# Aligned load targets, one output store, and half of a weight piece loaded by 8 DMA engines, in a one-core decode layer

## The chip, the core and the metric

The kernel runs on one NeuronCore of one Trainium2 chip. The metric is the device time of one execution, in microseconds (us). The kernel before takes 216.2 us (median of 4 runs, 216.03 to 216.39). SP, ACT, PE, DVE and POOL are the core's sync, scalar, tensor, vector and GpSimd engines; SP and ACT issue the loads and stores here. Where the text says 8 or 16 engines, or the late ones, it means the 16 DMA engines over which the profile gives its DMA share. A landing is one of the semaphore records with which a load or store reports its data as done: 16 for a load of a whole K, V, wo or w4 piece, fewer for some others (one more record that those have, at most 1.1 us after the start of the issue, is not counted). I read one landing as one engine's share; the end of the kernel before, below, fits that, but no record names an engine. The eviction is the copy of the result from PSUM to SBUF.

## The reference, cut to what matters

```python
def reference(A_x, A_k_cache, A_v_cache, A_wq, A_wo, B_x, B_w1, B_w2, B_w3, B_w4):
    # attention of 4 decode tokens, 32 query heads over 16 KV heads, last 2048 positions of the cache
    # q = (x @ wq); p = softmax(q k^T / sqrt(128)); o = p v; return o @ wo      wo: [4096, 576]
    # MLP: x + gelu(layernorm(x1) @ w3) @ w4        w3: [576, 4608], w4: [4608, 576]
    x = A_x
    xn = _layernorm(x, axis=-1)
    return x + _A_ref(xn, A_k_cache, A_v_cache, A_wq, A_wo) + _B_ref(xn, B_w1, B_w2, B_w3, B_w4)
```

With one position per token, the shifted-window part of the MLP adds nothing, so w1 and w2 are not read. All inputs are bf16. There are 16 K tiles and 16 V tiles of 2 MB each (one per KV head, for all four tokens), 4.7 MB each of wq and wo, and 5.3 MB each of w3 and w4.

## The kernel before

Loads go out on one queue, issued by SP, in a fixed order: x, wq, K0 to K2, then wo pieces, V and K tiles in turn, w3 after V2, and w4 last. A KV tile has 128 partitions of 16 KB; seven such buffers let SP issue far ahead of need (a K load lands a median of 29.3 us after its issue).

```python
    x_bf = const.tile([B, D], BF16)
    nc.sync.dma_start(out=x_bf[:], in_=x2)
    for j in range(KJ):                                  # wq: 4 pieces of 8192 B per partition
        nc.sync.dma_start(out=wq_sb[:, j * NQ:(j + 1) * NQ], in_=wq_main[:, j, :])
    ...
    wo_src = A_wo.rearrange("(s p i) n -> s p (i n)", p=P, i=WOR)     # WOR = WOH = 8

    def load_kv(kind, h):                                # source dimensions 32 x 4 x 8192
        t = kvp.tile([P, NC, Dh], BF16, tag="kv", name=f"{kind.lower()}n")
        nc.sync.dma_start(out=t[:].rearrange("p c d -> p (c d)"),
                          in_=win[:, h].rearrange("b (p c) d -> p b (c d)", c=NC))

    def load_wo(p):                                      # 128 partitions of 9216 B
        t = wop.tile([P, WOR, D], BF16, tag="wo", name="wo_sb")
        nc.sync.dma_start(out=t[:].rearrange("p i n -> p (i n)"), in_=wo_src[p])

    W4_PIECES = [0, NFH // 2, NFH, NFH + 9, NFH + 14, NF]             # rows of 1152 B; NFH = 18
```

In a wo piece, the 1024 rows belong to 8 heads of 128 channels. Partition p holds 8 consecutive rows, so the attention output has to be spread over the partitions in the same order. Eight matmuls with selection matrices do that (`o_spread`), and a mask keeps each partition's own head (`o_pick`). Whoever changes where the rows of a piece land must change both. The result is accumulated in four blocks of PSUM partitions and stored by four DMAs, two issued by SP and two by ACT:

```python
    fin = const.tile([P, CW], out.dtype)
    nc.vector.tensor_copy(out=fin[:], in_=acc[:])
    for i in range(NQD):
        eng = nc.sync if i % 2 == 0 else nc.scalar
        eng.dma_start(out=o2[:, i * CW:(i + 1) * CW], in_=fin[i * QD:i * QD + B, :])
```

Of the kernel before, what the change touches and what calls it, by code (L numbers as in the profile page):

```python
# [9 lines left out]
ALU = mybir.AluOpType  # L10
AX = mybir.AxisListType
BF16 = mybir.dt.bfloat16
F32 = mybir.dt.float32
I32 = mybir.dt.int32
PSUM = bass.MemoryType.PSUM

NKV = 7
BIG = 1.0e30


@with_exitstack
def kernel(
# [14 lines left out]
    nc = tc.nc  # L37
    P = 128
    B, Sq, D = A_x.shape
    _, Hkv, Sk, Dh = A_k_cache.shape  # L40
    Hq = A_wq.shape[1] // Dh
# [4 lines left out]
    KJ = 4  # L46
    NQ = Hq * Dh
    NF = F // P
    NFH = NF // 2
# [3 lines left out]
    QD = 32  # L53
    NQD = P // QD
    CG = NC // NQD
    NSL = 4
    SC = NC // NSL
    CW = D // NQD
# [7 lines left out]
    x2 = A_x.flatten_outer_dims()  # L66
    o2 = out.flatten_outer_dims()
# [2 lines left out]

    ctx.enter_context(tc.manual_schedule())

    const = ctx.enter_context(tc.tile_pool(name="const", bufs=1))
    small = ctx.enter_context(tc.tile_pool(name="small", bufs=2))
    kvp = ctx.enter_context(tc.tile_pool(name="kv", bufs=NKV))
    ktp = ctx.enter_context(tc.tile_pool(name="kt", bufs=3))
    ptp = ctx.enter_context(tc.tile_pool(name="pt", bufs=3))
    wp = ctx.enter_context(tc.tile_pool(name="w", bufs=1))
    wop = ctx.enter_context(tc.tile_pool(name="wo", bufs=2))
    ps_s = ctx.enter_context(tc.tile_pool(name="ps_s", bufs=3, space=PSUM))  # L80
    ps_o = ctx.enter_context(tc.tile_pool(name="ps_o", bufs=2, space=PSUM))
    ps_m = ctx.enter_context(tc.tile_pool(name="ps_m", bufs=1, space=PSUM))
    ps_acc = ctx.enter_context(tc.tile_pool(name="ps_acc", bufs=1, space=PSUM))


    x_bf = const.tile([B, D], BF16)
    nc.sync.dma_start(out=x_bf[:], in_=x2)

    wq_main = A_wq[0:KJ * P, :].rearrange("(p j) n -> p j n", j=KJ)
    wq_sb = wp.tile([P, KJ * NQ + NQ // 2], BF16, tag="w", name="wq_sb")  # L90
    for j in range(KJ):
        nc.sync.dma_start(out=wq_sb[:, j * NQ:(j + 1) * NQ], in_=wq_main[:, j, :])
    nc.sync.dma_start(out=wq_sb[:, KJ * NQ:], in_=A_wq[KJ * P:D, :].rearrange("r (e f) -> (r e) f", e=2))

    w_tiles = {}
    wo_tiles = {}
    kv_tiles = {}
    WOH = 8
    WOR = WOH
    WOD = P // WOH  # L100
    WOQ = WOH // rep
    wo_src = A_wo.rearrange("(s p i) n -> s p (i n)", p=P, i=WOR)

    def load_kv(kind, h):
# [3 lines left out]
                          in_=win[:, h].rearrange("b (p c) d -> p b (c d)", c=NC))  # L108
        kv_tiles[kind, h] = t

    def load_wo(p):
        t = wop.tile([P, WOR, D], BF16, tag="wo", name="wo_sb")
        nc.sync.dma_start(out=t[:].rearrange("p i n -> p (i n)"), in_=wo_src[p])
        wo_tiles[p] = t

    def load_w3():
# [4 lines left out]
        nc.sync.dma_start(out=t[:, KJ * F:], in_=B_w3[KJ * P:D, :].rearrange("r (e f) -> (r e) f", e=2))  # L121
        w_tiles["w3"] = t

    W4_PIECES = [0, NFH // 2, NFH, NFH + 9, NFH + 14, NF]

    def load_w4():
        t = wp.tile([P, NF, D], BF16, tag="w", name="w4_sb")
# [7 lines left out]
    ident_bf = const.tile([P, P], BF16)  # L135
    make_identity(nc, ident_bf[:])
    ident_f = const.tile([P, P], F32)
# [3 lines left out]
    neg_half = const.tile([B, 1], F32)  # L141
    nc.gpsimd.memset(neg_half[:], -0.5)

    AB = ps_acc.tile([P, 512], F32)
    nc.vector.memset(AB[:], 0.0)
    q_ps = AB[:, 0:Hq * B].rearrange("p (h b) -> p h b", b=B)
    g_ps = AB[:, Hq * B:Hq * B + NF * B].rearrange("p (f b) -> p f b", b=B)
    acc = ps_acc.tile([P, CW], F32)
# [18 lines left out]
    def transposed(src_bf, name):  # L167
        dup = small.tile([B, 2, P], BF16, tag="dup")
        nc.vector.memset(dup[:], 0.0)
        for e in range(2):  # L170
            nc.vector.tensor_copy(out=dup[:, e, e:P:2], in_=src_bf[:, KJ * P:D])
        T = const.tile([P, KJ + 2, B], BF16, name=name)
        tp = ps_m.tile([P, KJ + 2, B], BF16, tag="m")
        for j in range(KJ):
            nc.tensor.transpose(out=tp[:, j, :], in_=src_bf[:, j:KJ * P:KJ], identity=ident_bf[0:B, 0:B])
        for e in range(2):
            nc.tensor.transpose(out=tp[:, KJ + e, :], in_=dup[:, e, :], identity=ident_bf[0:B, 0:B])
        nc.vector.tensor_copy(out=T[:], in_=tp[:])
        return T

    xn_f = const.tile([B, D], F32)
    xn_bf = const.tile([B, D], BF16)
    layernorm(xn_f, xn_bf, x_bf)
    xnT = transposed(xn_bf, "xnT")


    for j in range(KJ):
        for h in range(Hq):
            nc.tensor.matmul(out=q_ps[:, h, :], lhsT=wq_sb[:, j * NQ + h * Dh:j * NQ + (h + 1) * Dh],
                             rhs=xnT[:, j, :], start=False, stop=False, skip_group_check=True)  # L190
    for h in range(Hq):
        e, f0 = divmod(h * Dh, NQ // 2)
        nc.tensor.matmul(out=q_ps[:, h, :], lhsT=wq_sb[:, KJ * NQ + f0:KJ * NQ + f0 + Dh],
                         rhs=xnT[:, KJ + e, :], start=False, stop=False, skip_group_check=True)
# [4 lines left out]
    for kb in range(NQD):  # L199
        nc.vector.tensor_copy(out=sel[:, :, :, kb, :],  # L200
                              in_=ident_bf[:].rearrange("p (ib i e) -> p ib e i", ib=2, e=2))
    qs_ps = ps_m.tile([P, 2, 2, Hkv, rep, B], F32, tag="m")
    for ib in range(2):
        for e in range(2):
            nc.tensor.matmul(out=qs_ps[:, ib, e].rearrange("p h r b -> p (h r b)"),
                             lhsT=sel[:, ib, e].rearrange("p k i -> p (k i)"), rhs=q_bf[:], start=True, stop=True)
    qz = const.tile([P, Hkv, 2, 2, NQD, B, rep], BF16)
    nc.gpsimd.memset(qz[:], 0.0)
    for kb in range(NQD):
        for ie in range(4):  # L210
            ib, e = divmod(ie, 2)
            nc.vector.tensor_copy(out=qz[kb * QD:(kb + 1) * QD, :, ib, e, kb, :, :],
                                  in_=qs_ps[kb * QD:(kb + 1) * QD, ib, e].rearrange("p h r b -> p h b r"))
# [9 lines left out]
    for r in range(rep):  # L223
# [1 line left out]
                                op0=ALU.add, op1=ALU.mult)  # L225


    sel_wo = const.tile([P, WOR, WOH, WOD], BF16)
    nc.gpsimd.tensor_copy(out=sel_wo[:], in_=ident_bf[:].rearrange("p (d i) -> p i d", i=WOR).unsqueeze(2)
                          .to_broadcast([P, WOR, WOH, WOD]))  # L230
    own = const.tile([P, WOH], F32)
    nc.vector.reduce_sum(out=own[:], in_=ident_f[:].rearrange("p (h d) -> p h d", h=WOH), axis=AX.X)

    xsum = const.tile([B, D], F32)
    nc.vector.tensor_tensor(out=xsum[:], in0=xn_f[:], in1=x_bf[:], op=ALU.add)
    for i in range(NQD):
        nc.tensor.matmul(out=acc[i * QD:i * QD + B, :], lhsT=ident_f[0:B, 0:B], rhs=xsum[:, i * CW:(i + 1) * CW],
                         start=False, stop=False, skip_group_check=True)
    ln2_bf = const.tile([B, D], BF16)
    layernorm(None, ln2_bf, xn_bf)  # L240
    ln2T = transposed(ln2_bf, "ln2T")
    gT = const.tile([P, NF, B], BF16)


    def acc_matmuls(lhsT, rhs):
        for i in range(NQD):
            nc.tensor.matmul(out=acc[i * QD:i * QD + B, :], lhsT=lhsT, rhs=rhs[:, i * CW:(i + 1) * CW],  # L247
                             start=False, stop=False, skip_group_check=True)

    kts = {}  # L250
    S_ps = {}
    PT = {}
    O_ps = {}
    st = {}

    def k_transpose(h, s):
        src = kv_tiles["K", h][:].bitcast(I32)[:, s * SC:(s + 1) * SC, :].rearrange("p c (ib i) -> p ib c i", i=QD)
        kt = ktp.tile([P, 2, SC, QD], I32, tag="kt")
        nc.vector.transpose(out=kt[:], in_=src)  # L259
        kts[h, s] = kt  # L260

    def k_mask(h):
        S_ps[h] = ps_s.tile([P, CG, NQD, NJ], F32, tag="S", name="S")
# [57 lines left out]
    def o_norm(h):  # L321
# [4 lines left out]
        nc.vector.reciprocal(out=rd[:], in_=dn[:])  # L326
        k = h % WOQ
        if k == 0:
# [5 lines left out]
    def o_spread(h):  # L334
        if h % WOQ < WOQ - 1:
            return
        on = st.pop("on")
        R = ps_m.tile([P, WOR, WOH, B], F32, tag="m", name="R")
        for i in range(WOR):
            nc.tensor.matmul(out=R[:, i].rearrange("p h b -> p (h b)"),  # L340
                             lhsT=sel_wo[:, i].rearrange("p h d -> p (h d)"),
                             rhs=on[:].rearrange("p h b -> p (h b)"), start=True, stop=True)
        st["R"] = R

    def o_pick(h):
        if h % WOQ < WOQ - 1:
            return
        mk = small.tile([P, WOR, WOH, B], BF16, tag="mk")
        nc.vector.tensor_tensor(out=mk[:], in0=st.pop("R")[:],
                                in1=own[:].unsqueeze(1).unsqueeze(3).to_broadcast([P, WOR, WOH, B]), op=ALU.mult)  # L350
        op = small.tile([P, WOR, B], BF16, tag="op")
        with nc.allow_low_precision("one term is not zero"):
            nc.vector.reduce_sum(out=op[:], in_=mk[:].rearrange("p i h b -> p i b h"), axis=AX.X)
        st["op"] = op

    def o_proj(h):
        if h % WOQ < WOQ - 1:
            return
        op = st.pop("op")
        for i in range(WOR):  # L360
            acc_matmuls(op[:, i, :], wo_tiles[h // WOQ][:, i, :])

# [10 lines left out]
    def mlp_act():  # L373
        xs = const.tile([P, NF, B], F32, name="g_x")
        nc.vector.tensor_copy(out=xs[:], in_=g_ps)  # L375
        u = const.tile([P, NF, B], F32, name="g_u")
        nc.vector.tensor_tensor(out=u[:], in0=xs[:], in1=xs[:], op=ALU.mult)
        nc.vector.tensor_scalar(out=u[:], in0=u[:], scalar1=GELU_A, scalar2=1.0, op0=ALU.mult, op1=ALU.add)
        nc.vector.tensor_tensor(out=u[:], in0=u[:], in1=xs[:], op=ALU.mult)
        nc.scalar.activation(out=u[:], in_=u[:], func=ACT.Tanh, scale=GELU_C)  # L380
        nc.vector.tensor_scalar(out=u[:], in0=u[:], scalar1=0.5, scalar2=0.5, op0=ALU.mult, op1=ALU.add)
        nc.vector.tensor_tensor(out=gT[:], in0=u[:], in1=xs[:], op=ALU.mult)

    def mlp_out(lo, hi):
        w4 = w_tiles["w4"]
# [92 lines left out]

    fin = const.tile([P, CW], out.dtype)
    nc.vector.tensor_copy(out=fin[:], in_=acc[:])  # L480
    for i in range(NQD):
        eng = nc.sync if i % 2 == 0 else nc.scalar
        eng.dma_start(out=o2[:, i * CW:(i + 1) * CW], in_=fin[i * QD:i * QD + B, :])


# [28 lines left out]
```

## Time and profile before

| | before |
|---|---|
| median time | 216.2 us |
| span of the profiled run | 214.6 us |
| read from HBM | 87.17 MB |
| rate in the middle of the span | about 428 GB/s |
| PE / DVE busy | 56% / 55% |
| last data landing, end | 210.21, 214.6 us |

From the page of the kernel before, the span and the last two rows of the table of 40 slices (each slice is 5.4 us; DMA is the busy share of the 16 DMA engines in tenths, GB/s what they moved):

```profile
span 214.6 us, 6449 instructions
DMA  5999999999999999999999999999999999999960
GB/s 207 429 437 434 428 429 425 425 425 437 426 429 423 437 431 419 439 425 434 431 428 425 428 428 430 422 434 431 429 418 428 437 419 425 437 427 422 419 262 12
```

The stream is full from slice 2 to 38. No engine is near full; this kernel is bound by its loads. The end of the chain that ended last (start, duration, what):

```profile
152.04 30.72 DMA kn<-in_A_k_cache_dram
182.76 0.02 issue
182.78 27.43 DMA w_sb<-in_B_w_dram
210.21 0.04 issue
210.26 0.68 PE acc L247 x16
210.93 0.02 issue
210.96 0.31 DVE fin L480
```

Only one microsecond of compute follows the last load (0.68 and 0.31 us). So I count what ends the stream earlier at its full size, an estimate from this chain. The end of the stream itself is ragged. This is the view of windows of the kernel before (window, its length, then busy us and instructions of PE, PE weight loads, DVE, ACT, POOL, the granted PE clock, the DMA share and GB/s):

```profile
core 0: us, PE busy (x) PEld busy (x) DVE busy (x) ACT busy (x) POOL busy (x), PEclk, DMA share, GB/s
165.00:170.00 5.00, 3.76 (x83) 2.54 (x80) 3.27 (x5) 0.33 (x2) 0.00 (x0) 1.00 1.02 428
170.00:175.00 5.00, 1.61 (x56) 1.50 (x53) 2.95 (x6) 3.96 (x15) 0.00 (x0) 1.00 1.01 430
175.00:180.00 5.00, 2.03 (x43) 1.44 (x44) 0.00 (x0) 0.00 (x0) 0.00 (x0) 1.00 1.02 436
...
205.00:206.00 1.00, 0.98 (x45) 0.78 (x38) 0.09 (x1) 0.00 (x0) 0.00 (x0) 1.00 0.68 285
206.00:207.00 1.00, 0.00 (x0) 0.00 (x0) 0.00 (x0) 0.00 (x0) 0.00 (x0) 1.00 0.55 228
207.00:208.00 1.00, 0.73 (x36) 0.58 (x36) 0.00 (x0) 0.00 (x0) 0.00 (x0) 1.00 0.53 220
208.00:209.00 1.00, 0.12 (x8) 0.12 (x11) 0.00 (x0) 0.00 (x0) 0.00 (x0) 0.88 0.41 158
209.00:210.00 1.00, 0.65 (x20) 0.44 (x13) 0.00 (x0) 0.00 (x0) 0.00 (x0) 0.50 0.18 74
```

From 206 us on, the DMA share is 0.55 and less. The semaphore records of the trace say the same: the last w4 piece has 16 landings, here in us after the first. From 207 to 208 us, when seven and then eight of them are past, the share is 0.53.

```
before, first at 205.50:  0.00 0.12 0.15 0.20 0.23 0.26 1.05 1.82 | 3.14 3.28 3.33 4.24 4.46 4.57 4.65 4.71
```

Eight engines are early and eight late. The spread grows through the run: 0.56 us in the first wq load; 1.58 us in the first K tile, behind the first 16 KB packet of instructions (a fetch, at 15.0 us); 4.71 us at the end. The lags behind the first landing add up to 4.2 us in that wq load and to 36.2 us in the last w4 piece. The difference of 32 us is about what the trace has for it: 22 packets of instructions of 0.88 to 0.98 us (20.6 us in all) and 11.9 us of longer data packets, 22 of those 26 beside a fetch. The trace does not say which engine carried a packet.

### The profile page before, as it was taken

The numbers are of one execution on the slowest core, as the hardware profiler recorded it, in microseconds if no ns is written. First come the engines' busy times: TensorE is split into PE (matmuls) and PEld (weight loads), VectorE is DVE, ScalarE is ACT, GpSimd is POOL, SyncE is SP. The second block draws the span as 40 slices with busy tenths as digits, with TensorE's granted clock in tenths as the row PEclk, the third lists the DMA queues.
The fourth block names the chain that finished last, engine by engine and source line by source line (L and its number), as shares of the span: only waits on it lengthen the run. The fifth ranks groups of instructions, "written<-read, shape, count | busy, mean of one in ns | idle before, by whom it ended". The sixth has DMA issues, their size and how long they took to land. (4 is left out here: it accounts for less than half of the span.)

```text
span 214.6 us, 6449 instructions
## 1 busy us (share of the span) xinstructions
PE 121.0 (56%) x2893; PEld 94.9 (44%) x2893; DVE 118.0 (55%) x223; ACT 70.1 (33%) x258; POOL 6.1 (3%) x14
## 2 busy tenths in 40 slices
PE   0461355647470017157999577677474705779752
PEld 0350143445360015145899456555453604557641
DVE  5608799766470047348610798785573924854210
ACT  0000005571634001607070045570725340709600
POOL 5400100000000000000000000000000000000000
PEclk9999999999999999999999999999999999999995
DMA  5999999999999999999999999999999999999960
GB/s 207 429 437 434 428 429 425 425 425 437 426 429 423 437 431 419 439 425 434 431 428 425 428 428 430 422 434 431 429 418 428 437 419 425 437 427 422 419 262 12
DMA packets 7123, 87.58 MB, mean 408 GB/s; under 512 B 820, under 2 KB 824, under 8 KB 1336
## 3 DMA queue, kind: packets, MB, share of 16 engines
q1 hardware_dynamic: 7080, 87.17, 95.7%
q8 instruction: 22, 0.36, 0.6%
q14 instruction: 5, 0.04, 0.0%
q10 hardware_dynamic: 16, 0.00, 0.0%
HBM read 87.17 MB, written 0.00 MB: 406 GB/s over the span
## 5 line engine op out<-in xcount | busy, mean ns | idle before, releaser
L302 ACT ACTIVATE pt<-S 32x128 bf16<-32x128 f32 x256 | 68.5, 268 | 92.0 <-issue 55.3
L259 DVE STREAM_TRANSPOSE kt<-kn 128x1024 int32<-128x1024 int32 x64 | 74.3, 1205 | 11.4 <-DMA kn<-in_A_k_cache_dram 11.4
L313 PE MATMUL O<-pt,vn 128*128 128x8 bf16 x1024 | 37.4, 169 | 43.2 <-DMA vn<-in_A_v_cache_dram 41.7
L313 PEld LDWEIGHTS <-vn 128*128 128x128 bf16 x1024 | 34.4, 105 | 51.3 <-DMA vn<-in_A_v_cache_dram 43.6
L273 PE MATMUL S<-qz,kt 128*128 128x32 bf16 x1024 | 39.1, 189 | 25.2 <-DVE kt L259 25.2
L273 PEld LDWEIGHTS <-kt 128*128 128x128 bf16 x1024 | 33.6, 106 | 36.1 <-DVE kt L259 30.4
L287 DVE TENSOR_REDUCE m<-mxT 8x1 f32<-8x128 f32 x16 | 4.4, 277 | 42.6 <-PE mxT L285 42.6
L316 PE MATMUL O<-pt,ones_bf 128*128 128x64 bf16 x128 | 17.1, 226 | 0.0
L302 ACT ACT_TABLE_LOAD x1 | 1.3, 1283 | 32.6 <-DVE mx L280 32.6
L368 PEld LDWEIGHTS <-w_sb 128*128 128x128 bf16 x144 | 11.4, 164 | 0.5 <-issue 0.4
L368 PE MATMUL AB<-ln2T,w_sb 128*128 128x4 bf16 x144 | 11.5, 202 | 0.0
L280 DVE TENSOR_REDUCE mx<-S 128x8 f32<-128x512 f32 x16 | 10.4, 652 | 1.0 <-PE S L273 1.0
L295 PE MATMUL S<-dg,ones_bf 8*128 8x512 bf16 x16 | 9.6, 601 | 0.1
L265 PE MATMUL S<-negbig,ohT 4*128 4x512 bf16 x16 | 9.6, 601 | 0.0
L316 PEld LDWEIGHTS <-ones_bf 128*128 128x128 bf16 x128 | 8.4, 104 | 0.0
L370 PE MATMUL AB<-ln2T,w_sb 128*128 128x4 bf16 x36 | 7.3, 202 | 0.0
L247 PE MATMUL acc<-w_sb,gT 128*4 128x144 bf16 x144 | 4.8, 294 | 2.8 <-DMA w_sb<-in_B_w_dram 2.8
L324 DVE TENSOR_REDUCE dn<-O 128x8 f32<-128x64 f32 x16 | 3.3, 208 | 5.5 <-PE O L316 5.5
L375 DVE COPY g_x<-AB 128x144 f32<-128x144 f32 x1 | 0.3, 307 | 10.7 <-PE AB L370 10.7
L285 PE MATMUL mxT<-ident_f,mx 128*8 128x128 f32 x16 | 6.0, 374 | 0.3 <-DVE mx L280 0.3
L370 PEld LDWEIGHTS <-w_sb 128*128 128x128 bf16 x36 | 5.9, 165 | 0.0
L247 PEld LDWEIGHTS <-gT 128*4 128x4 bf16 x144 | 3.4, 104 | 3.6 <-issue 3.5
(72 smaller groups left out, 64.9 us busy)
## 6 DMA issues: line engine op xcount, KB each, us to landing
kn<-in_A_k_cache_dram SPq DMA_DIRECT2D x16, 2048.0 KB, 29.3
vn<-in_A_v_cache_dram SPq DMA_DIRECT2D x16, 2048.0 KB, 27.0
wo_sb<-in_A_wo_dram SPq DMA_DIRECT2D x4, 1152.0 KB, 28.8
w_sb<-in_B_w_dram SPq DMA_DIRECT2D x2, 2304.0 KB, 31.8
wq_sb<-in_A_wq_dram SPq DMA_DIRECT2D x4, 1024.0 KB, 4.9
w_sb<-in_B_w_dram SPq DMA_DIRECT2D x3, 1296.0 KB, 32.8
w_sb<-in_B_w_dram SPq DMA_DIRECT2D x2, 576.0 KB, 32.2
w_sb<-in_B_w_dram SPq DMA_DIRECT2D x1, 720.0 KB
```

What stands on the lines that cost most here:

```text
L247: nc.tensor.matmul(out=acc[i * QD:i * QD + B, :], lhsT=lhsT, rhs=rhs[:, i * CW:(i + 1) * CW], start=False, stop=False, skip_group_check=True)
L259: nc.vector.transpose(out=kt[:], in_=src)
L265: nc.tensor.matmul(out=S_ps[h][:].rearrange("p g k j -> p (g k) j"), lhsT=ohT[:], rhs=nb, start=True, stop=False, skip_group_check=True)
L273: nc.tensor.matmul(out=S_ps[h][:, s * (SC // NQD) + g].rearrange("p k j -> p (k j)"), lhsT=kt[:, ib, g * NQD:(g + 1) * NQD, e:2 * QD:2].re ...
L280: nc.vector.reduce_max(out=mx[:], in_=S_ps[h][:].rearrange("p g k j -> p j (g k)"), axis=AX.X)
L285: nc.tensor.transpose(out=mxT[:], in_=st[h][:], identity=ident_f[:])
L295: nc.tensor.matmul(out=S_ps[h][:].rearrange("p g k j -> p (g k) j"), lhsT=ones_bf[0:NJ, :], rhs=dg, start=False, stop=False, skip_group_ch ...
L302: nc.scalar.activation(out=PT[h][kb * QD:(kb + 1) * QD, :, c4, :], in_=S_ps[h][c4 * QD:(c4 + 1) * QD, :, kb, :], func=ACT.Exp, scale=scale)
L313: nc.tensor.matmul(out=O_ps[h][:, 0:NJ], lhsT=vn[:, g * NQD + s, :], rhs=pt[:, g, s, :], start=(g == 0 and s == 0), stop=False, skip_group ...
L316: nc.tensor.matmul(out=O_ps[h][:, NJ:].rearrange("p (c j) -> p c j", j=NJ), lhsT=ones_bf[:], rhs=pt[:, g:g + DG, s, :], start=False, stop= ...
L368: nc.tensor.matmul(out=g_ps[:, i, :], lhsT=w3[:, j * F + e * (F // 2) + f0:j * F + (e + 1) * (F // 2):NFH], rhs=ln2T[:, j, :], start=False ...
L370: nc.tensor.matmul(out=g_ps[:, i, :], lhsT=w3[:, KJ * F + f0:KJ * F + F // 2:NFH], rhs=ln2T[:, KJ + e, :], start=False, stop=False, skip_g ...
```

## The change

The intent has three parts. Load targets are put at multiples of 256 bytes: the pools of load targets move to the front behind a pad, and w4 is cut at even rows. The output goes out in one store, for which every accumulation writes 32 columns with the four tokens 8 rows apart. And the ragged end is to be evened out: half of the last wo piece is loaded by only 8 DMA engines, with its own selection matrices and mask. The start is also rearranged (x issued on ACT, wq in two pieces).

```diff
+PAD = 96
+    pad.tile([P, PAD], F32, name="pad")
+    ... pools kv, w, wo, kt, pt now come before const and small ...
-    nc.sync.dma_start(out=x_bf[:], in_=x2)
+    nc.scalar.dma_start(out=x_bf[:], in_=x2)
-    for j in range(KJ):
-        nc.sync.dma_start(out=wq_sb[:, j * NQ:(j + 1) * NQ], in_=wq_main[:, j, :])
+    for e in range(2):
+        lo, hi = e * 2 * NQ, (e + 1) * 2 * NQ
+        nc.sync.dma_start(out=wq_sb[:, lo:hi], in_=wq_main[:, lo:hi])
+    wo_half = A_wo.rearrange("(s h a d i) n -> s a h d (i n)", h=WOH, a=2, d=WOD, i=WOR // 2)
     def load_wo(p):
+        if p < Hq // WOH - 1:
             nc.sync.dma_start(out=t[:].rearrange("p i n -> p (i n)"), in_=wo_src[p])
+        else:
+            nc.sync.dma_start(out=t[:, 0:WOR // 2, :].rearrange("p i n -> p (i n)"),
+                              in_=wo_half[p, 0].rearrange("h d n -> d h n"))
+            nc.sync.dma_start(out=t[:, WOR // 2:, :].rearrange("p i n -> p (i n)"), in_=wo_half[p, 1])
-    W4_PIECES = [0, NFH // 2, NFH, NFH + 9, NFH + 14, NF]
+    W4_PIECES = [0, 10, NFH, NFH + 10, NFH + 14, NF]
+    ... fill_sel(last), own[:, 2 variants]; op and gT 32 columns wide, tokens at every 8th ...
-    for i in range(NQD):
-        eng = nc.sync if i % 2 == 0 else nc.scalar
-        eng.dma_start(out=o2[:, i * CW:(i + 1) * CW], in_=fin[i * QD:i * QD + B, :])
+    nc.sync.dma_start(out=o2.rearrange("b (i n) -> i b n", i=NQD), in_=fin[0:P:RS, :])
```

In the first half (source dimensions 16 x 8), partition 8d + h gets channel group d of head h. In the second (8 x 16), partition 16h + d does.

More of the change, by code (lines that the diff above doesn't have):

```diff
@@ L71 @@
     ctx.enter_context(tc.manual_schedule())
+    pad = ctx.enter_context(tc.tile_pool(name="pad", bufs=1))
+    pad.tile([P, PAD], F32, name="pad")
+    kvp = ctx.enter_context(tc.tile_pool(name="kv", bufs=NKV))
+    wp = ctx.enter_context(tc.tile_pool(name="w", bufs=1))
+    wop = ctx.enter_context(tc.tile_pool(name="wo", bufs=2))
+    ktp = ctx.enter_context(tc.tile_pool(name="kt", bufs=3))
+    ptp = ctx.enter_context(tc.tile_pool(name="pt", bufs=3))
     const = ctx.enter_context(tc.tile_pool(name="const", bufs=1))
     small = ctx.enter_context(tc.tile_pool(name="small", bufs=2))
-    kvp = ctx.enter_context(tc.tile_pool(name="kv", bufs=NKV))
-    ktp = ctx.enter_context(tc.tile_pool(name="kt", bufs=3))
-    ptp = ctx.enter_context(tc.tile_pool(name="pt", bufs=3))
-    wp = ctx.enter_context(tc.tile_pool(name="w", bufs=1))
-    wop = ctx.enter_context(tc.tile_pool(name="wo", bufs=2))
     ps_s = ctx.enter_context(tc.tile_pool(name="ps_s", bufs=3, space=PSUM))
@@ L83 @@
     ps_acc = ctx.enter_context(tc.tile_pool(name="ps_acc", bufs=1, space=PSUM))
-    x_bf = const.tile([B, D], BF16)
-    nc.sync.dma_start(out=x_bf[:], in_=x2)
-    wq_main = A_wq[0:KJ * P, :].rearrange("(p j) n -> p j n", j=KJ)
-    wq_sb = wp.tile([P, KJ * NQ + NQ // 2], BF16, tag="w", name="wq_sb")
-    for j in range(KJ):
-        nc.sync.dma_start(out=wq_sb[:, j * NQ:(j + 1) * NQ], in_=wq_main[:, j, :])
-    nc.sync.dma_start(out=wq_sb[:, KJ * NQ:], in_=A_wq[KJ * P:D, :].rearrange("r (e f) -> (r e) f", e=2))
     w_tiles = {}
@@ L109, in load_kv @@
         kv_tiles[kind, h] = t
+    x_bf = const.tile([B, D], BF16)
+    nc.scalar.dma_start(out=x_bf[:], in_=x2)
+    wq_sb = wp.tile([P, KJ * NQ + NQ // 2], BF16, tag="w", name="wq_sb")
+    wq_main = A_wq[0:KJ * P, :].rearrange("(p j) n -> p (j n)", j=KJ)
+    for e in range(2):
+        lo, hi = e * 2 * NQ, (e + 1) * 2 * NQ
+        nc.sync.dma_start(out=wq_sb[:, lo:hi], in_=wq_main[:, lo:hi])
+    nc.sync.dma_start(out=wq_sb[:, KJ * NQ:], in_=A_wq[KJ * P:D, :].rearrange("r (e f) -> (r e) f", e=2))
     def load_wo(p):
         t = wop.tile([P, WOR, D], BF16, tag="wo", name="wo_sb")
-        nc.sync.dma_start(out=t[:].rearrange("p i n -> p (i n)"), in_=wo_src[p])
+        if p < Hq // WOH - 1:
+            nc.sync.dma_start(out=t[:].rearrange("p i n -> p (i n)"), in_=wo_src[p])
+        else:
+            nc.sync.dma_start(out=t[:, 0:WOR // 2, :].rearrange("p i n -> p (i n)"),
+                              in_=wo_half[p, 0].rearrange("h d n -> d h n"))
+            nc.sync.dma_start(out=t[:, WOR // 2:, :].rearrange("p i n -> p (i n)"), in_=wo_half[p, 1])
         wo_tiles[p] = t
@@ L142 @@
     nc.gpsimd.memset(neg_half[:], -0.5)
+    RS = QD // B
     AB = ps_acc.tile([P, 512], F32)
@@ L184, with k_transpose @@
     xnT = transposed(xn_bf, "xnT")
+    kts = {}
+    def k_transpose(h, s):
+        src = kv_tiles["K", h][:].bitcast(I32)[:, s * SC:(s + 1) * SC, :].rearrange("p c (ib i) -> p ib c i", i=QD)
+        kt = ktp.tile([P, 2, SC, QD], I32, tag="kt")
+        nc.vector.transpose(out=kt[:], in_=src)
+        kts[h, s] = kt
     for j in range(KJ):
@@ L225 @@
                                 op0=ALU.add, op1=ALU.mult)
-    sel_wo = const.tile([P, WOR, WOH, WOD], BF16)
-    nc.gpsimd.tensor_copy(out=sel_wo[:], in_=ident_bf[:].rearrange("p (d i) -> p i d", i=WOR).unsqueeze(2)
-                          .to_broadcast([P, WOR, WOH, WOD]))
-    own = const.tile([P, WOH], F32)
-    nc.vector.reduce_sum(out=own[:], in_=ident_f[:].rearrange("p (h d) -> p h d", h=WOH), axis=AX.X)
-    xsum = const.tile([B, D], F32)
+    hr = WOR // 2
+    sel_wo = const.tile([P, WOR, P], BF16)
@@ new lines, in fill_sel @@
+    def fill_sel(last):
+        if not last:
+            nc.gpsimd.tensor_copy(out=sel_wo[:].rearrange("p i (h d) -> p i h d", h=WOH),
+                                  in_=ident_bf[:].rearrange("p (d i) -> p i d", i=WOR).unsqueeze(2)
+                                  .to_broadcast([P, WOR, WOH, WOD]))
+            return
+        halves = ident_bf[:].rearrange("p (a d i) -> p a i d", a=2, i=hr)
+        nc.gpsimd.tensor_copy(out=sel_wo[:, 0:hr].rearrange("p i (d h) -> p i d h", h=WOH),
+                              in_=halves[:, 0].unsqueeze(3).to_broadcast([P, hr, WOD, WOH]))
+        nc.gpsimd.tensor_copy(out=sel_wo[:, hr:].rearrange("p i (h d) -> p i h d", h=WOH),
+                              in_=halves[:, 1].unsqueeze(2).to_broadcast([P, hr, WOH, WOD]))
@@ new lines @@
+    fill_sel(False)
+    own = const.tile([P, 2, WOR, WOH], BF16)
+    with nc.allow_low_precision("sums of zeros and a one"):
+        by_h = small.tile([P, 2, WOH], BF16, tag="by_h")
+        nc.vector.reduce_sum(out=by_h[:, 0], in_=ident_f[:].rearrange("p (h d) -> p h d", h=WOH), axis=AX.X)
+        nc.vector.reduce_sum(out=by_h[:, 1], in_=ident_f[:].rearrange("p (d h) -> p h d", h=WOH), axis=AX.X)
+    nc.vector.tensor_copy(out=own[:, 0], in_=by_h[:, 0].unsqueeze(1).to_broadcast([P, WOR, WOH]))
@@ L235 @@
+    nc.vector.tensor_copy(out=own[:, 1, 0:hr], in_=by_h[:, 1].unsqueeze(1).to_broadcast([P, hr, WOH]))
+    nc.vector.tensor_copy(out=own[:, 1, hr:], in_=by_h[:, 0].unsqueeze(1).to_broadcast([P, hr, WOH]))
+    idz = const.tile([B, QD], F32)
+    nc.gpsimd.memset(idz[:], 0.0)
+    nc.gpsimd.tensor_copy(out=idz[:, 0:QD:RS], in_=ident_f[0:B, 0:B])
+    xsum = xn_f
     nc.vector.tensor_tensor(out=xsum[:], in0=xn_f[:], in1=x_bf[:], op=ALU.add)
     for i in range(NQD):
-        nc.tensor.matmul(out=acc[i * QD:i * QD + B, :], lhsT=ident_f[0:B, 0:B], rhs=xsum[:, i * CW:(i + 1) * CW],
+        nc.tensor.matmul(out=acc[i * QD:(i + 1) * QD, :], lhsT=idz[:], rhs=xsum[:, i * CW:(i + 1) * CW],
@@ L241 @@
     ln2T = transposed(ln2_bf, "ln2T")
-    gT = const.tile([P, NF, B], BF16)
+    gT = const.tile([P, NF, QD], BF16)
+    nc.gpsimd.memset(gT[:], 0.0)
+    op = const.tile([P, WOR, QD], BF16)
+    nc.gpsimd.memset(op[:], 0.0)
     def acc_matmuls(lhsT, rhs):
         for i in range(NQD):
-            nc.tensor.matmul(out=acc[i * QD:i * QD + B, :], lhsT=lhsT, rhs=rhs[:, i * CW:(i + 1) * CW],
+            nc.tensor.matmul(out=acc[i * QD:(i + 1) * QD, :], lhsT=lhsT, rhs=rhs[:, i * CW:(i + 1) * CW],
                              start=False, stop=False, skip_group_check=True)
-    kts = {}
     S_ps = {}
@@ L254 @@
     st = {}
-    def k_transpose(h, s):
-        src = kv_tiles["K", h][:].bitcast(I32)[:, s * SC:(s + 1) * SC, :].rearrange("p c (ib i) -> p ib c i", i=QD)
-        kt = ktp.tile([P, 2, SC, QD], I32, tag="kt")
-        nc.vector.transpose(out=kt[:], in_=src)
-        kts[h, s] = kt
     def k_mask(h):
@@ L340, in o_spread @@
             nc.tensor.matmul(out=R[:, i].rearrange("p h b -> p (h b)"),
-                             lhsT=sel_wo[:, i].rearrange("p h d -> p (h d)"),
+                             lhsT=sel_wo[:, i],
                              rhs=on[:].rearrange("p h b -> p (h b)"), start=True, stop=True)
         st["R"] = R
+        if h // WOQ == Hq // WOH - 2:
+            fill_sel(True)
     def o_pick(h):
@@ L349, in o_pick @@
         nc.vector.tensor_tensor(out=mk[:], in0=st.pop("R")[:],
-                                in1=own[:].unsqueeze(1).unsqueeze(3).to_broadcast([P, WOR, WOH, B]), op=ALU.mult)
-        op = small.tile([P, WOR, B], BF16, tag="op")
+                                in1=own[:, h // (Hkv - 1)].unsqueeze(3).to_broadcast([P, WOR, WOH, B]), op=ALU.mult)
         with nc.allow_low_precision("one term is not zero"):
-            nc.vector.reduce_sum(out=op[:], in_=mk[:].rearrange("p i h b -> p i b h"), axis=AX.X)
-        st["op"] = op
+            nc.vector.reduce_sum(out=op[:, :, 0:QD:RS], in_=mk[:].rearrange("p i h b -> p i b h"), axis=AX.X)
     def o_proj(h):
@@ L358, in o_proj @@
             return
-        op = st.pop("op")
         for i in range(WOR):
@@ L381, in mlp_act @@
         nc.vector.tensor_scalar(out=u[:], in0=u[:], scalar1=0.5, scalar2=0.5, op0=ALU.mult, op1=ALU.add)
-        nc.vector.tensor_tensor(out=gT[:], in0=u[:], in1=xs[:], op=ALU.mult)
+        nc.vector.tensor_tensor(out=gT[:, :, 0:QD:RS], in0=u[:], in1=xs[:], op=ALU.mult)
     def mlp_out(lo, hi):
```

## The prediction

> **What bounds the kernel.** The DMA stream. The 40-slice table shows the DMA engines at 9 tenths or more from slice 2 to 37, at 418 to 439 GB/s for 87.17 MB; PE is busy 56%, DVE 55% of the 214.6 us span. The chain of waits ends with 27.4 us of w4 DMA, 0.68 us of matmuls, the 0.31 us eviction, and 3.3 us for store and end. SP issues over 20 us ahead of the landings, so the stream never starves.
>
> **Where the stream loses.**
> 1. *Unequal engines.* The 16 landings of the last w4 piece (semaphore records) spread from 205.50 to 210.21 us: six within 0.3 us, then +1.05 and +1.82, and eight at +3.14 to +4.71. DMA share by 1 us windows agrees: 0.68, 0.55, 0.53, 0.41, 0.18 from 205 to 210. The spread grows by about 1 us at each of 22 instruction packets of 16 KB (packet records, q8; a data packet beside one takes about 1107 instead of 611 ns). They seem to go to one half of the engines.
> 2. *Start.* wq is issued behind x on SP: at 1.16 instead of 0.73 us.
> 3. *Packets.* Each data packet takes bytes/27.2 GB/s plus 8.2 ns (16384 B: 611; 8192: 309; 4608: 178).
>
> **Alignment: almost nothing.** [...] But the compiled addresses before already put all kv, wq, w3 and wo tiles at multiples of 256; the padding only keeps that in the new order. Only two w4 pieces (rows 9 to 17, 27 to 31) start at 128 mod 256, and their packets (389, 220 ns) follow the rule of the aligned ones: the trace shows no cost. [...]
>
> **What the change is worth.**
> - wo half on 8 engines: [...] Per engine, eight packets of 178 ns, and sixteen more on eight engines, replace eight of 347: +1.5 us on the loaded half, -1.35 us on the other. If the loaded half is the early one, the last landing moves by -1.35 us. Critical in full.
> - x on ACT, wq first on SP: -0.43 us, critical.
> - wq in two packets per row, not four: 16 packets per engine less, -0.13 us.
> - One store: last landing 213.09, first SP store's 212.64: -0.4 us.
> - Added: 32-column weight loads, memsets, second filling of the selection matrices, mask copies: off the critical path, about 0.
>
> Sum -2.3 us: 213.85; with the risks I say **213.9 us**, range 212.5 to 215.5. Chances: faster by over 2% 0.05, within 2% 0.94, slower 0.01.
>
> **Checks in the profile after.** First wq packet near 1.7 us; last w4 landings spread about 1.8 to 2 us, the last near 208.3; 178 and 611 ns packets unchanged; GB/s in the middle unchanged (about 428); the store lands about 1.7 us after the eviction.
>
> **What would make it wrong.** (a) The loaded engines are the late half: +1.5 us. (b) [...] packets stretch: the 1.35 us gone, 215.2. (c) Alignment matters after all[...]. (d) Instruction fetches move to other engines.

-1.35, -0.43, -0.13, -0.4 and about 0 come to -2.31 us, the -2.3 of the text.

## The result, and the profile after

The kernel after takes 222.3 us (median of 4 runs, 221.22 to 222.87). The ratio to before is 1.0275, with a 95% interval of 1.0241 to 1.031. (A ratio here is the mean time of one kernel's fast runs over that of the other's of the same rounds, so not quite the ratio of the medians quoted.) It is slower by 6 us where 2.3 us less was predicted.

The same rows of the page, for the kernel after:

```profile
span 220.0 us, 6458 instructions
DMA  7999999999999999999999999999999999999970
GB/s 242 429 429 429 429 441 418 432 426 429 435 423 425 435 423 438 423 432 429 426 429 426 425 433 435 429 429 429 429 423 251 226 333 435 429 422 426 423 291 7
```

The busy row looks as full as before. The row below it does not: slices 31 to 33 (165 to 181 us) moved 251, 226 and 333 GB/s. The engines were occupied but moved little more than half. The windows of the kernel after show the stretch more closely:

```profile
160.00:165.00 5.00, 2.28 (x66) 1.83 (x62) 2.52 (x6) 3.66 (x14) 0.00 (x0) 1.00 1.02 433
165.00:170.00 5.00, 3.76 (x93) 2.87 (x93) 3.90 (x5) 0.95 (x4) 0.00 (x0) 1.00 0.99 252
170.00:175.00 5.00, 0.97 (x35) 0.86 (x31) 1.67 (x2) 3.35 (x13) 0.00 (x0) 1.00 1.06 223
175.00:180.00 5.00, 0.00 (x0) 0.00 (x0) 0.66 (x4) 0.00 (x0) 0.00 (x0) 1.00 0.99 295
180.00:185.00 5.00, 0.96 (x19) 0.66 (x19) 0.00 (x0) 0.00 (x0) 0.00 (x0) 1.00 1.01 433
```

DMA share 1.0 at half the GB/s means that each packet takes twice as long. The packet records show it. Elsewhere, but for single packets beside an instruction fetch, a 16384 B packet takes 611 ns and one of 4608 B takes 178 ns. Of the packets that start between 170 and 175 us, all 29 of 16384 B take 1036 ns or more and all 139 of 4608 B take 218 ns or more, with medians of 1120 and 341 ns. The 4608 B packets in this stretch are the halves of the last wo piece. The chain that ended last shifted with the stream:

```profile
151.67 37.16 DMA kn<-in_A_k_cache_dram
188.83 0.02 issue
188.85 26.87 DMA w_sb<-in_B_w_dram
215.72 0.04 issue
215.76 0.70 PE acc L292 x12
216.46 0.02 issue
216.48 0.31 DVE fin L517
```

The wait for the last K tile grew from 30.72 to 37.16 us, 6.4 us more. The w4 part behind it did not grow (27.43, then 26.87 us). All of the loss arises before 189 us. The end is also not evened out: the landings of the last w4 piece are spread over 5.64 us instead of 4.71 (two come 2.4 us before the next one). The last still comes 2.4 us after their mean, as before (2.37 and 2.45).

Two small parts can be read directly. The first wq packet starts at 1.745 us instead of 2.146. And the store saves nothing. This is the timeline of its issues, before and then after (start, duration, engine):

```profile
211.29 0.63 SPq L483 DMA_DIRECT2D out_dram<-fin  x2
211.30 0.92 ACTq L483 DMA_DIRECT2D out_dram<-fin  x2
```

```profile
216.82 0.65 SPq L518 DMA_DIRECT2D out_dram<-fin  x1
```

One store over 4 x 4 rows takes as long to issue (0.65 us) as two stores of 4 rows (0.63 us). Counted from the end of the eviction, the last store landing comes after 213.09 - 211.27 = 1.82 us before and after 218.57 - 216.79 = 1.78 us after.

### The profile page after: what moved, and what is told of

Same layout as the page of the kernel before. It is cut to its first block, busy times and chain, and to the rows that moved or that the text cites. A ratio compares the mean times of both kernels' runs of the same rounds, so it can differ in the third digit from the quotient of the medians.

```text
span 220.0 us, 6458 instructions
## 1 busy us (share of the span) xinstructions
PE 120.7 (55%) x2893; PEld 95.2 (43%) x2893; DVE 119.8 (54%) x227; ACT 70.4 (32%) x258; POOL 9.3 (4%) x20
## 5 line engine op out<-in xcount | busy, mean ns | idle before, releaser
L258 POOL COPY sel_wo<-ident_bf 128x512 bf16<-128x512 bf16 x1 | 0.6, 611 | 162.2 <-PE R L378 162.2
L292 PE MATMUL acc<-w_sb,gT 128*32 128x144 bf16 x144 | 4.5, 286 | 2.3 <-DMA w_sb<-in_B_w_dram 2.3
## 6 DMA issues: line engine op xcount, KB each, us to landing
wq_sb<-in_A_wq_dram SPq DMA_DIRECT2D x2, 2048.0 KB, 11.9
```

Of the source, the lines that this page charges most:

```text
L292: nc.tensor.matmul(out=acc[i * QD:(i + 1) * QD, :], lhsT=lhsT, rhs=rhs[:, i * CW:(i + 1) * CW], start=False, stop=False, skip_group_check= ...
```

## The experiments

To follow how much of a loss comes from stretched packets, I add up, over all data packets from 4 KB on and from 14 us on, the time beyond the usual time of their size, where it is over 60 ns. Some 12 engine-microseconds of this are there in every kernel, in before mostly from packets beside instruction fetches (10.8 of 11.9). Divided by the 16 engines, the rest is my estimate of what stretching costs the stream. A check from other records: the mean of the last w4 piece's 16 landings came 6.0 us later in the run after than in a_whole (5.9 by this sum), and 6.1 us later in d_odd than in before (4.8 by this sum, and 1.2 for the bytes that d_odd adds, 8 x 2.45 us over 16 engines).

| run | median us | stretch, engine-us | beyond 12, over 16 engines |
|---|---|---|---|
| before | 216.2 | 11.9 | 0 |
| after | 222.3 | 106.9 | 5.9 |
| a_whole | 215.54 | 12.3 | 0 |
| b_half | 221.73 | 105.4 | 5.8 |
| a_both16 | 220.79 | 95.6 | 5.2 |
| a_both8 | 225.86 | 149.9 | 8.6 |
| a_32x4 | 215.95 | 12.2 | 0 |
| d_own | 218.03 | 12.3 | 0 |
| d_odd | 221.69 | 89.5 | 4.8 |
| d_two | 222.16 | 78.5 | 4.2 |

The medians of before in the three batches were 216.15 (a_whole, b_half, a_both16, a_both8), 216.33 (d_own, d_odd, d_two, b_mis224) and 216.35 us (the rest). The four runs not listed (d_low4, b_mis224, b_mis128, b_start) have 12.0 to 12.4. Every run was correct. By the record's line of 2%, after, b_half, a_both8, d_odd and d_two are slower, a_both16 is unclear (its interval, 1.0199 to 1.023, holds the line), and all others are the same as before; what is said below of differences under 2% rests on intervals that leave out 1.

Differences of half a microsecond need one more look. From the last store landing to the end of the program takes 1.46 or 1.47 us in before, after and five other runs, but 1.08 in a_whole, 0.97 in b_half, 0.93 or 0.94 in the four runs with extra loads and 1.64 in b_start. Why is open. So for small gains I compare when the last w4 piece has landed: 210.21 us in before.

The expectations speak of a theory P. It is that the copies of the halved piece slow the stream by where they write; P8 says that only the half on 8 engines does it, P16 that the half on 16 does it too. The theory also said which engine writes which partitions, and why that should cost time. No record names the engine of a packet.

### Is it the halved piece, and nothing else? (a_whole, b_half)

The kernel after, with its last piece loaded whole:

```diff
-        if p < Hq // WOH - 1:
+        if True:
-        if h // WOQ == Hq // WOH - 2:
-            fill_sel(True)
-                                in1=own[:, h // (Hkv - 1)]...
+                                in1=own[:, 0]...
```

> The kernel after with its last wo piece loaded whole by 16 engines, as the first three. Theory P ([...] slows the stream from 166 to 179 us): no packet over 600 ns for 4608 B, GB/s stays near 428 there, and the time is the rest of the change, 215.2 to 215.7 us. Rival R (the time went elsewhere: later loads, the new order of the pools, the second filling of the selection matrices): stays over 219 us.

It took 215.54 us, ratio 0.997 (0.9955 to 0.9985), and its last w4 piece landed at 209.77 us. The slow slices are gone:

```profile
GB/s 246 439 420 414 439 425 430 439 429 426 440 417 424 426 435 422 433 435 426 426 426 435 426 424 428 432 426 429 417 429 430 420 441 435 420 426 424 425 281 21
```

The kernel before, with only the halved piece, its matrices and masks, and 224 bytes of padding ahead of the load targets (otherwise the larger constants would push the targets to 32 mod 256):

> The kernel before with the halves of the last wo piece alone (its matrices and masks, and 224 bytes of padding so that all tiles stay at multiples of 256). Theory P: the whole loss, 216.2 + 6 to 7 = 222 to 223.5 us, with the same stretch of half the GB/s. Rival R: about 216.2, or 214.9 if the shift of load works as predicted.

It took 221.73 us, ratio 1.0273 (1.0249 to 1.0297), the loss of the whole change. So the two halves cost some 6 us, and the rest of the change is worth -0.6 us, of which the stream shows 0.44 (209.77 against 210.21); the shorter end after the last store is the other part. The version without the halves beats both kernels, though the one before only by 0.3%.

### Which of the two halves? (a_both16, a_both8)

Both halves of the last piece with source dimensions 16 x 8, on 16 engines; matrices and mask are filled to match:

```diff
-            nc.sync.dma_start(out=t[:, WOR // 2:, :]..., in_=wo_half[p, 1])
+            nc.sync.dma_start(out=t[:, WOR // 2:, :]..., in_=wo_half[p, 1].rearrange("h d n -> d h n"))
```

> The kernel after with both halves loaded in the d-h order by 16 engines. Theory P8 (the copy on 8 engines is at fault[...]): no slow stretch, 215.2 to 215.7 us. Rival P16 (already the first half[...], or reading rows at a wide pitch, is at fault): two slow stretches, 219 us or more.

Both halves with source dimensions 8 x 16, on 8 engines:

```diff
-                              in_=wo_half[p, 0].rearrange("h d n -> d h n"))
+                              in_=wo_half[p, 0])
```

> The kernel after with both halves loaded by 8 engines. Theory P8: about twice the slow stretch, 215.5 + 2 x 6.5 = 226 to 230 us, late landings of the 8 engines. Rival P16: less slow than after, under 221 us, for the d-h half is gone.

The first took 220.79 us (ratio 1.0214), the second 225.86 us (1.0453), just under the range expected from P8. In the landing records, a half with source dimensions 16 x 8 has 16 landings and one with 8 x 16 has 8, so, with a landing read as an engine, the counts of engines are as intended. The theory that only the copy on 8 engines is at fault falls: with both halves on 16 engines, the stream is slow just the same. Both kinds of half are at fault, the one on 8 engines more (8.6 us of stream for two of them, against 5.2). The windows of a_both16:

```profile
165.00:170.00 5.00, 3.76 (x91) 2.81 (x91) 3.85 (x5) 0.88 (x4) 0.00 (x0) 1.00 1.03 252
170.00:175.00 5.00, 1.03 (x37) 0.93 (x33) 1.28 (x3) 3.42 (x13) 0.00 (x0) 1.00 1.02 220
175.00:180.00 5.00, 0.00 (x0) 0.00 (x0) 1.09 (x5) 0.00 (x0) 0.00 (x0) 1.00 1.01 367
```

For a_both16 the sum from stretching, 5.2 us, is all of its distance to a_whole (220.79 - 215.54 = 5.25 us).

### The disputed cost by itself: target partitions or source? (d_own, d_odd, d_two)

Which engine writes which partitions, no record says. I chose the targets by a supposition about that; what the runs test is whether the target partitions matter at all.

So the kernel before got four extra loads ahead of V12, each of 8 rows of 16 KB, into a spare turn of the KV buffers; nothing reads them. Source, size and count are the same in all three runs. Only the target partitions differ:

```diff
+            if (kind, h) == ("V", 12):
+                extra = kvp.tile([P, NC, Dh], BF16, tag="kv", name="extra")
+                for j in range(4):
+                    nc.sync.dma_start(out=extra[TARGET].rearrange("p c d -> p (c d)"),
+                                      in_=k_win[j, 0, 0:8 * NC, :].rearrange("(p c) d -> p (c d)", c=NC))
# d_own:  TARGET = j:29 + j:4            partitions j, j+4 .. j+28
# d_odd:  TARGET = 64 + j:64 + 29 + j:4  the same, 64 higher
# d_two:  TARGET = 8 * j:8 * j + 8       8 neighbours
```

> The kernel before plus four extra loads (131 KB each, never read) [...]to partitions j, j+4 .. j+28[...]. Theory P[...]: those 8 engines lose 4 x 611 ns = 2.45 us each and stay behind no one: time 216.2 to 216.6, no packet of 16384 B stretched. [...] Rival H (HBM or the use of only 8 engines is the cost, not the target partitions): +2 us or more and the same as the next two.

> The same with partitions 64+j .. 64+j+28[...], packets of 16384 B at about 1220 ns for some 5 us[...]: about 218.6. Rival H: the same as d_own.

> The same with 8 neighbouring partitions in each load (8j .. 8j+7)[...]: 221 to 224 us. Rival H: the same as d_own.

The 216.2 to 216.6 us of d_own are for the case that the loaded engines are the early ones.

They took 218.03, 221.69 and 222.16 us (ratios 1.0062, 1.0253, 1.0272). Each extra load has eight data landings in all three traces. The windows of d_own and then d_odd:

```profile
170.00:172.00 2.00, 1.44 (x51) 1.33 (x48) 1.46 (x2) 1.89 (x8) 0.00 (x0) 1.00 1.01 431
172.00:174.00 2.00, 0.00 (x0) 0.00 (x0) 1.32 (x5) 1.91 (x8) 0.00 (x0) 1.00 1.05 448
174.00:176.00 2.00, 0.00 (x0) 0.00 (x0) 0.00 (x0) 0.02 (x1) 0.00 (x0) 1.00 0.99 426
```

```profile
170.00:172.00 2.00, 1.49 (x52) 1.38 (x49) 1.79 (x3) 1.89 (x8) 0.00 (x0) 1.00 1.11 233
172.00:174.00 2.00, 0.00 (x0) 0.00 (x0) 1.04 (x4) 1.91 (x8) 0.00 (x0) 1.00 1.00 234
174.00:176.00 2.00, 0.00 (x0) 0.00 (x0) 0.00 (x0) 0.07 (x1) 0.00 (x0) 1.00 0.93 201
```

And one window of d_two:

```profile
170.00:175.00 5.00, 1.33 (x48) 1.22 (x44) 2.67 (x6) 3.72 (x14) 0.00 (x0) 1.00 1.04 216
```

Between 170 and 175 us, none of 111 packets of 16384 B is stretched in d_own, and all 47 are in d_odd (from 611 ns to a median of 1221), as are all 40 in d_two. The rival (HBM reads, or the use of few engines) would have made the three alike; it falls. What costs is where the copy writes: between d_own and d_odd nothing else in the program differs. (Whether the eight landings are of the same eight engines in all three, the traces do not show.) The effect is larger than I expected. For d_odd I had reckoned with 2.4 us (218.6); every 16384 B packet of those 5 us stretched, and it lost 5.4 us. d_two fell into its expected range, but I had expected it to stretch more than d_odd, and it stretched less (4.2 against 4.8 us). So my estimates of the size do not hold.

d_own held a second surprise. No packet was stretched beyond the usual, and yet it lost 1.7 us (its last w4 piece landed 2.36 us later). The landings of the last w4 piece, in us after the first:

```
before   0.00 0.12 0.15 0.20 0.23 0.26 1.05 1.82 | 3.14 3.28 3.33 4.24 4.46 4.57 4.65 4.71
d_own    0.00 0.37 2.34 2.63 2.79 2.99 3.05 3.11   3.39 3.63 4.33 4.45 4.68 4.80 7.05 7.10
```

Each of the engines that took the extra loads should move by 4 x 611 ns = 2.45 us. Two of the early landings stayed, and two landings came at 7.05 and 7.10, where before had none later than 4.71. So of the 8 loaded engines, six were early and two were late, and the two late ones now end the stream. The landings of the first extra load say the same directly: 169.3, 169.5, 169.6, 169.7, 170.6 and 171.4 us, and two at 172.4. The eight loaded engines are not the early eight. Even without any stretching, moving work to these 8 engines lengthened the end (the last landing came 2.36 us later). (One of the four runs of d_own took 216.5 us, the others 218.0 to 218.2. Only one of the slower ones was profiled, so why is open.)

### Which engines are early? (d_low4)

The same with four target rows, meant for four engines:

```diff
-extra[j:29 + j:4] ... k_win[j, 0, 0:8 * NC, :]
+extra[j:13 + j:4] ... k_win[j, 0, 0:4 * NC, :]
```

> As the extra loads to partitions j, j+4 .. but only four of them, j .. j+12[...]. [...] 216.2 to 216.5 us, four of the early landings of the last w4 piece move by 2.45 us and none passes +5. [...] 218 us and one or two landings at +7.1. No packet stretches in either case.

The first outcome is for the case that the two late engines of d_own are not among the four loaded here, the second for the case that late ones are among them.

It took 215.8 us, ratio 0.9976 (0.9963 to 0.999): four times 64 KB more are read, and nothing is lost. Four early landings moved by 2.5 us (the sequence is now 0.00 0.13 0.36 0.84 2.57 2.75 2.94 2.97 ... 4.95). The first extra load landed at 169.5, 169.7, 170.5 and 171.2 us, none as late as the two of d_own. So the four loaded engines are early ones. The stream is not faster than before: the last landing came 0.21 us later, at 210.42. The time is shorter because the program ended 0.94 us after its last store landing instead of 1.47.

### Can a halved piece be loaded without the cost? (a_32x4)

The kernel after, with the last piece halved by heads instead of by channels. Both halves then have source dimensions 32 x 4, as the K and V loads have. They keep 4608 B per packet and 16 engines. Matrices and mask are filled to match:

```diff
-    wo_half = A_wo.rearrange("(s h a d i) n -> s a h d (i n)", h=WOH, a=2, d=WOD, i=WOR // 2)
+    wo_half = A_wo.rearrange("(s g h d i) n -> s g d h (i n)", g=2, h=WOH // 2, d=2 * WOD, i=WOR // 2)
```

> The kernel after with the last wo piece halved by heads instead of by channels: both halves have source dimensions 32 x 4, as the K and V loads have, on 16 engines, with the same packets of 4608 B as the run with both halves at 16 x 8. Theory P[...]: no slow stretch, 215.5 us. Rival W (halving, or short packets read at a wide pitch, is the cost): slow stretch as before, about 220.8.

It took 215.95 us, ratio 0.998 (0.9966 to 0.9994), and its windows show no trace of the stretch:

```profile
165.00:170.00 5.00, 3.76 (x93) 2.87 (x93) 3.90 (x5) 0.94 (x4) 0.00 (x0) 1.00 0.99 410
170.00:175.00 5.00, 0.97 (x35) 0.86 (x31) 2.32 (x5) 3.35 (x13) 0.00 (x0) 1.00 1.04 442
```

Beside a_both16 this is the closest pair: the same piece in packets of the same size on 16 engines, and only the shape of the source differs, 16 x 8 against 32 x 4. (The outer rows of the source also lie 9216 B apart in the one and 4608 B in the other, so this pair alone does not rule out the reads; d_own against d_odd, which read the same bytes, does for the extra loads.) How either shape is dealt out over the engines, the trace does not show: it names no engine for a packet.

### Alignment by itself (b_mis224, b_mis128)

The compiled addresses put all load tiles of the kernel before at multiples of 256 already (the KV tiles start at 38144 = 149 x 256). So alignment can be tested only by taking it away, with a pad of 224 or 128 bytes ahead of the kernel's load targets:

```diff
+    pad = ctx.enter_context(tc.tile_pool(name="pad", bufs=1))
+    pad.tile([P, 56], F32, name="pad")      # b_mis128: 32
     kvp = ctx.enter_context(tc.tile_pool(name="kv", bufs=NKV))
```

> The kernel before with 224 bytes of padding ahead of the load targets: all start at 224 mod 256 instead of 0. [...] By my reading of the packets of the two shifted w4 pieces: 611 ns, 216.2 us.

> The kernel before with all load targets at 128 mod 256. [...] If the cost seen at 224 (packets of 614 to 621 ns, +2.1 us) comes only near the end of a 256-byte block, as the unchanged packets of the two shifted w4 pieces suggest: 611 ns, 216.2 us.

| targets at, mod 256 | median us | ratio | mean time of a 16384 B packet, ns |
|---|---|---|---|
| 0 (before) | 216.3 | 1 | 611.0 |
| 128 | 217.72 | 1.0062 | 614.1 |
| 224 | 218.44 | 1.0095 | 615.7 |

(The mean is over packets below 700 ns.) Alignment does cost: per packet 3.1 ns at 128 and 4.7 ns at 224, and 1.4 and 2.1 us in all. Both expectations, no cost at either offset, were wrong: at 128 nearly all packets take 611 to 622 ns, with a median of 613.

### The start by itself (b_start)

```diff
-    nc.sync.dma_start(out=x_bf[:], in_=x2)
+    nc.scalar.dma_start(out=x_bf[:], in_=x2)
-    for j in range(KJ): ...                # wq in 4 pieces
+    for e in range(2): ...                 # wq in 2 pieces
```

> The kernel before with x issued on ACT and wq in two pieces instead of four, nothing else. By the prediction -0.43 and -0.13 us: 215.6 us, first wq packet near 1.74 us. The run without the wo halves gave -0.6 for all parts but the halves, and its store landed as late after the eviction as that of before, so this part should be all of it.

It took 215.85 us, ratio 0.9977 (0.9964 to 0.9989), that is -0.5 us. The time alone proves little, since d_low4 gained as much at its end. But the last w4 piece landed at 209.74 us, 0.47 us earlier than in before; in a_whole it is 0.44 and in a_32x4 0.42 us. So the start is about all that the useful part of the change amounts to.

## Why the prediction was wrong

**The step that failed.** "If the loaded half is the early one, the last landing moves by -1.35 us. Critical in full." Two things were wrong with it.

- *The cost of the new copies.* I listed it as risk (b), "packets stretch: the 1.35 us gone, 215.2". The stretch was named, though only as a risk outside the number, and its size was wrong: I took it to use up the gain, and it cost 5.9 us of stream (94.6 engine-us of stretching more than in a_whole, over 16 engines), because every packet in the stretch took longer. d_own against d_odd shows that the target partitions can cause it; a_both16 against a_32x4 shows that it can happen with 16 landings too. The mechanism that I gave for it is shown by no run.
- *The early half.* "They seem to go to one half of the engines" was inferred from the count, eight and eight. It does not hold for the eight engines that d_own loaded: it put two landings at +7.05 and +7.10. If the half piece runs on the same eight, which no trace shows, the +1.5 us on the loaded engines would have ended the stream an estimated 1.5 us later, even without stretching. In the profile after, this second error can't be told from the first: the last w4 piece landed 5.95 us later than in a_whole (215.72 against 209.77), which the stretching alone accounts for. The profiled runs are 6.4 us apart (221.85 against 215.49); the other 0.4 us lies after the last store landing.

**The other terms.**

- *Start, -0.43, and wq packets, -0.13:* together -0.56 predicted, -0.5 measured (b_start), and -0.42 to -0.47 in the last landing of the three runs that share it. The first wq packet came at 1.745 us, as said (1.795 in b_start).
- *One store, -0.4:* wrong. It landed 1.78 us after the eviction, against 1.82 before. I had taken the landing of the first of two stores as that of one store, but the larger store is issued for 0.65 us instead of 0.29.
- *Alignment, almost nothing:* right for this change, because the targets were aligned before it (a_whole and b_start landed their last w4 piece within 0.03 us of each other). "The trace shows no cost" was wrong as a general reading. It rested on the median packets of two shifted w4 pieces, and shifting all targets costs 1.4 to 2.1 us.
- *Off the critical path, about 0* (32-column weight loads, masks, matrices): right; they are all still in a_32x4, whose last w4 piece landed at 209.79 us. (a_whole has no second filling.)

**What stays open.** Why every packet in such a stretch takes longer is not settled; no run here separates the causes. Nor was the evening-out achieved. In before, the landings of the last piece average 2.26 us after the first and the last comes at 4.71, so perfect balance would save an estimated 2.4 us. By the landings of d_own, however, two of the eight late engines are among the eight that it loaded and six are not, and no layout tried here takes bytes from just the late ones.

## What to carry to other kernels

In these runs the stream kept its full rate with halves of 32 x 4 (a_32x4) and with extra loads to every fourth of the lowest 32 partitions (d_own) or of the lowest 16 (d_low4): 418 to 448 GB/s from 170 us on. It fell to about half, 182 to 234 GB/s, with halves of 16 x 8 or 8 x 16 (after, b_half, a_both16, a_both8), and with the same extra loads to partitions 64 higher (d_odd) or to 8 neighbours (d_two): in after, 590 KB of each half cost 5.9 us of stream. Before you give a copy an unusual shape (8 or 16 outer rows, partition slices), test that shape alone beside one whose rate you have measured, and look for DMA share near 1 with falling GB/s: busy engines moving half was the mark of it here. Before you shift load from late engines to early ones, find out which they are by giving a few of them known extra work, and test the shift alone.
